# Sums of x made earlier, take-outs ahead of the curve, joined blocks in PSUM, parts in halves: one change to a retention kernel with two MLP layers

## The chip, the cores and the metric

The kernel runs on one core of one Trainium2 chip. The metric is the device time of one execution in microseconds (us). TensorE (PE) does the matmuls, VectorE (DVE), ScalarE (ACT) and GpSimd (POOL) do the elementwise work, and SyncE (SP) issues the DMAs. Each engine works through its own list of instructions in order and waits where an operand or a buffer isn't ready.

## The reference

```python
def _attn_ref(q, k, v):                      # 2 batches, 8 heads, 768 tokens, head size 64
    for t in range(S):
        state = gamma * state + einsum('bhd,bhe->bhde', k[:, :, t], v[:, :, t])
        y[:, :, t] = scale * einsum('bhd,bhde->bhe', q[:, :, t], state)

x = attn_out as 1536 tokens x 512
h = x @ w_in;  g = softplus(h);         x = g @ w_out      # layer one, 512 -> 2048 -> 512
h = x @ w_in2; g = s * relu(h)**2 + b;  y = g @ w_out2     # layer two
```
The softplus is written as max(h, 0) + log1p(exp(-|h|)). All data are float32.

## The kernel before

**Parts.** A matmul operand is kept as a high part (rounded by ScalarE) and a low part (the rest, a subtraction, mostly on GpSimd by `split`, L112 and L115); each product is three matmuls: high by high, high by low, low by high. `xh`, `xl` are the parts of x; `wh`, `wl` of the weights; `gh`, `gl` of the curve's result. The weights come as 64 bit words and are put together on VectorE (L287, L291, L296, L302) before their parts are made.

**Tiles.** The 1536 tokens are three tiles j of 512. The 2048 hidden units are 16 blocks of 128. PSUM has the banks `h`, `y` and `third` for first products, `word` for the weights, and four banks `acc` for second products, which are taken out into `xa[j]` when a tile's sum over some blocks is done. While one tile's sum is built, the one before must have left the same four banks.

**Stages.** (1) The recurrence over chunks of 128 tokens, with the first eight of twelve `step`s of layer one between its units (`early`, `mixed`). (2) The last four steps of these twelve, without recurrence. The first group of blocks is taken out by ScalarE (L412 in `take_out`), later ones are added into `xa` by VectorE (L590 in `take_2`). (3) `plain(0, P0)`: one pair of blocks, six slots (three tiles by two blocks), each a first product, its curve and a second product. (4) `second(0, p)` for three pairs: the first products of tiles 0 and 1 are made by a Strassen-like scheme with seven instead of eight half products, from sums of w (`sums_w`, `split_sums`) and sums of x; six slots again, each `part`, matmuls, `begin`, `middle`, the second products of another block (`whole`: `acc_2`, then `take_2`), `finish`. (5) Twelve ordinary steps. (6) Layer two: `plain(1, 0)` and `second(1, p)` for seven pairs.

**Sums of x.** `sum_x0` makes them for layer one: k = 1 on GpSimd in three rounds (L471), k = 2 on VectorE (L474, L475, twice as wide), k = 4 and k = 3 on VectorE, four instructions each (L465). `parts_x` makes their parts (L483 or L485, L488). They go into `xa[2]` and into two tiles called `p5` and `u2`. `all_x0` hands out one round for each `next(sums_0)`: one in each step of stage 2, k = 4 in slot 0 of `plain(0, P0)`, k = 3 in slot 1. `sum_x` is the same for layer two.

**The curve of a pair in layer one.** `begin` takes relu on ScalarE (L533), `middle` makes -2 relu(h) + h on VectorE (L545) and its softplus on ScalarE (L546), `finish` adds both on GpSimd (L554). Blocks of which one half product was kept in SBUF (`kept`, L508) are first added together by `joined` (L519).

The order on each engine is the order of the code: `tc.manual_schedule()` changes nothing in it.

Of the kernel before, what the change touches and what calls it, by code (L numbers as in the profile page):

```python
# [7 lines left out]
F32 = mybir.dt.float32  # L8
# [3 lines left out]
ALU = mybir.AluOpType  # L12
# [29 lines left out]
P0, P1 = FG // 2, PAIRS - FG // 2  # L42
# [6 lines left out]
def tile_retention_mlps(ctx: ExitStack, tc: tile.TileContext, qk, kv, w1, w2, sb, consts, out):  # L49
    nc = tc.nc  # L50
# [59 lines left out]
    def split(hi, lo, src, hi_eng, lo_eng):  # L110
        if hi_eng is nc.scalar:
            nc.scalar.activation(hi, src, AF.Copy)  # L112
        else:
            hi_eng.tensor_copy(hi, src)
        lo_eng.tensor_tensor(out=lo, in0=src, in1=hi.bitcast(F32), op=ALU.subtract)  # L115
# [210 lines left out]
    def split_sums(w):  # L326
        hi = late.tile([P, 4, KH], F32R, tag="sh", name="sh")
        lo = late.tile([P, 4, KH], F32R, tag="sl", name="sl")
        split(hi, lo, s_t[w], nc.scalar, nc.gpsimd)
        s_t[w] = (hi, lo)  # L330
        yield

# [118 lines left out]
    def sum_x0(k):  # L451

        def of(j, half):
            return [t[j][:, 2 * half : 2 * half + 2].bitcast(F32) for t in (xh, xl)]

        add, less = ALU.add, ALU.subtract
        (h11, l11), (h12, l12), (h21, l21), (h22, l22) = of(0, 0), of(1, 0), of(0, 1), of(1, 1)
        if k > 2:
            for c, tag in enumerate(("p5", "u2")):
                x3[c] = late.tile([P, TT], F32, tag=tag, name=tag)  # L460
            t, t2 = x3, x_t[2]
            todo = ((t2, h11, less), (None, l11, less)) if k == 3 else ((h21, t2, less), (None, l21, add))
            for x, y, op in todo:
                for c in range(2):
                    nc.vector.tensor_tensor(out=t[c], in0=t[c] if x is None else x[:, c], in1=y[:, c], op=op)  # L465
            return
        t = x_t[k] = xa[2][:, 2 * k - 2 : 2 * k]
        if k == 1:
            for x, y, op in ((h12, h11, less), (t, l12, add), (t, l11, less)):
                for c in range(2):  # L470
                    nc.gpsimd.tensor_tensor(out=t[:, c], in0=x[:, c], in1=y[:, c], op=op)  # L471
                yield
        else:
            nc.vector.tensor_tensor(out=t, in0=h22, in1=x_t[1], op=less)  # L474
            nc.vector.tensor_tensor(out=t, in0=t, in1=l22, op=add)  # L475
            yield

    def parts_x(k, la=1):
        hi, lo = both(k)
        if k == 3 or k == 4 and not la:  # L480
            src = [x3[c] for c in range(2)]
            for c in range(2):
                nc.scalar.activation(hi[:, c], src[c], AF.Copy)  # L483
        else:
            nc.scalar.activation(hi, x_t[k], AF.Copy)  # L485
            src = [x_t[k][:, c] for c in range(2)]
        for c in range(2):
            nc.gpsimd.tensor_tensor(out=lo[:, c], in0=src[c], in1=hi[:, c].bitcast(F32), op=ALU.subtract)  # L488
        x_t[k] = hi, lo

    def six(ps, w, x, start):
# [21 lines left out]
    def next_t():  # L513
        turn[0] ^= 1
        return tp.tile([P, TT], F32, tag="t2" if turn[0] else "t1", name="c")

    def joined(ps, t):
        c = next_t()
        nc.vector.tensor_tensor(out=c, in0=ps, in1=t, op=ALU.add)  # L519
        return c  # L520

    def begin(la, src, own=False, by_pool=True, tags=None):

        if la:
            c = src if own else next_t()
            nc.scalar.activation(c, src, AF.Relu)  # L526
            return src, c, None
        if tags:
            r, u = (late.tile([P, TT], F32, tag=tag, name=tag) for tag in tags)
        else:  # L530
            r, u = next_t(), None
        if by_pool:
            nc.scalar.activation(r, src, AF.Relu)  # L533
            return src, r, u if tags else src if own else next_t()
        nc.vector.tensor_scalar(
            out=r.bitcast(U32), in0=src.bitcast(U32), scalar1=0x80000000, scalar2=None, op0=ALU.bitwise_or
        )
        nc.scalar.activation(r, r, AF.Softplus)
        return src, r, None
# [169 lines left out]
    with tc.manual_schedule():  # L709
# [57 lines left out]
        def mixed(s):  # L767
# [18 lines left out]
                    take_out(old, cc)  # L786
            fill(2)

        for s in range(SB):
            (early if s < LAG_U else mixed)(s)  # L790
        for old in range(SB - LAG_U, SB - LAG):
            acc_mm(old, FIRST)
            acc_mm(old, SECOND)
# [13 lines left out]
        def go_first():  # L807
            if work not in sums_of_w:
                go(work, 2)
# [49 lines left out]
        def whole(acc, take):  # L859
            acc(FIRST + SECOND)  # L860
            take(FIRST + SECOND)
# [29 lines left out]
        def second(la, p):  # L891

            w = la * NF + 2 * p
            base = at[la, p + 1]
            (ah, al), (bh, bl), (sh, sl) = w_t[w, 0], w_t[w + 1, 0], s_t[w]
            a11, a12 = (ah[:, :KH], al[:, :KH]), (ah[:, KH:], al[:, KH:])
            a22 = bh[:, KH:], bl[:, KH:]
            s1, s2, s3, s4 = ((sh[:, k], sl[:, k]) for k in range(4))
            b11, b21 = ((xh[0][:, k : k + 2], xl[0][:, k : k + 2]) for k in (0, 2))
            b22 = xh[1][:, 2:4], xl[1][:, 2:4]  # L900
            t1, t2, t3, n4 = (x_t[k] for k in (1, 2, 3, 4))

            one, other, third = bank(ps_h, "h"), bank(ps_y, "y"), bank_2[1]

            part(base + 2)
            six(one, a11, b11, True)
            p1 = kept(one, "p1")
            six(third, a12, b21, True)
            c11 = begin(la, joined(third, p1), own=True)
            end_part()  # L910
            go_first()
            middle(c11)
            whole(*of_pair(la, p - 1, 1, 0))
            finish(la, p, 0, 0, c11)
            go_last()

            part(base + 3)
            six(other, s1, t1, True)
            p5 = kept(other, "p5")
            six(one, s2, t2, False)  # L920
            u2 = kept(one, "u2")
            end_part()
            go_first()
            whole(*of_pair(la, p - 1, 1, 1))
            go_last()

            part(base + 4)
            six(other, s4, b22, False)
            c12 = begin(la, joined(other, u2), own=True)
            six(one, s3, t3, False)  # L930
            c22 = begin(la, joined(one, p5), own=True)
            end_part()
            go_first()
            middle(c12)
            middle(c22)
            whole(*of_pair(la, p - 1, 2, 0))
            finish(la, p, 0, 1, c12)
            finish(la, p, 1, 1, c22)
            go_last()

            part(base + 5)
            six(one, a22, n4, False)
            c21 = begin(la, one, tags=("u2", "p1"))
            end_part()
            go_first()
            middle(c21)
            whole(*of_pair(la, p - 1, 2, 1))
            finish(la, p, 1, 0, c21)
            go_last()

            part(base + 6)
            all_of(third, (ah, al), 2)
            ha = begin(la, third)
            end_part()
            go_first()
            middle(ha)
            whole(*of_pair(la, p, 0, 0))
            finish(la, p, 0, 2, ha)
            go_last()

            part(base + 7)
            other = bank(ps_y, "y")
            all_of(other, (bh, bl), 2)
            hb = begin(la, other)
            end_part()
            go_first()
            middle(hb)
            for banks in (FIRST, SECOND) if la and p == PAIRS - 1 else (FIRST + SECOND,):
                acc_2(la, p, 0, 1, banks)
                take_2(la, p, 0, banks)  # L970
            finish(la, p, 1, 2, hb)
            go_last()

        def all_x0():
            for k in (1, 2, 4, 3):
                yield from sum_x0(k)
                if k > 2:
                    yield

        def all_x():  # L980
            for k in (1, 3, 2, 4):
                sum_x(k)
                yield

        sums_0 = all_x0()
        for s in range(SB, GS):
            accs = [of_step(s - LAG)]
            step(s, accs, at[0, P0 + 1] * (s < SB + 2), [sums_0], nc.gpsimd)
        s = GS - 1
        act_3(s)  # L990
        act_hi(s)
        act_lo(s, nc.gpsimd)
        parts_x(1, 0)
        left = [lambda s=s: whole(*of_step(s)) for s in range(GS - LAG, GS)]
        plain(0, P0, left, [[sums_0], [sums_0], [], [], [], []], [(4,), (2,), (), (3,), (), ()])
        for p in range(P0 + 1, P1):
            second(0, p)
        end_part()
# [103 lines left out]
```

## Time and profile before

| what | value |
|---|---|
| time, median of 3 runs | 585.71 us (585.37 to 586.18) |
| profiled execution: its own time, its span | 586.1 us, 584.0 us |
| PE busy in the span | 565.4 us (97%) |
| DVE, ACT, POOL busy | 411.0, 337.5, 340.8 us |
| mean granted TensorE clock | 0.993 of full speed |

The span goes from the first to the last instruction of the profile; the 2.1 us between it and the time lie outside. PE is busy nearly everywhere, so what can be won without taking matmuls away is in its 18.6 idle us and in the stretches where its clock is lowered.

### The profile page before, as it was taken

The numbers are of one execution on the slowest core, as the hardware profiler recorded it, in microseconds if no ns is written. First come the engines' busy times: TensorE is split into PE (matmuls) and PEld (weight loads), VectorE is DVE, ScalarE is ACT, GpSimd is POOL, SyncE is SP. The second block draws the span as 40 slices with busy tenths as digits, with TensorE's granted clock in tenths as the row PEclk, the third lists the DMA queues.
The fourth block names the chain that finished last, engine by engine and source line by source line (L and its number), as shares of the span: only waits on it lengthen the run. The fifth ranks groups of instructions, "written<-read, shape, count | busy, mean of one in ns | idle before, by whom it ended". The sixth has DMA issues, their size and how long they took to land.

```text
span 584.0 us, 8106 instructions
## 1 busy us (share of the span) xinstructions
PE 565.4 (97%) x2968; PEld 462.7 (79%) x2968; DVE 411.0 (70%) x619; ACT 337.5 (58%) x606; POOL 340.8 (58%) x276
## 2 busy tenths in 40 slices
PE   8899999996999999999999999999999999999997
PEld 7777778885878877788887887888888888888885
DVE  4899766497796968999697687667576665765324
ACT  4656564434554454654344697858676666667460
POOL 3447634885769696963344769756464655556030
PEclk9999999997999999999999999999999999999999
DMA  8985212102021221233210213222212122100005
GB/s 334 415 303 198 70 50 96 37 1 74 17 91 37 72 74 65 82 106 101 81 50 23 73 36 109 72 74 64 81 36 93 52 73 72 37 0 1 0 2 215
DMA packets 14870, 50.58 MB, mean 87 GB/s; under 512 B 1776, under 2 KB 1776, under 8 KB 14832
## 3 DMA queue, kind: packets, MB, share of 16 engines
q1 hardware_dynamic: 14832, 50.08, 25.0%
q8 instruction: 23, 0.38, 0.2%
q14 instruction: 15, 0.12, 0.1%
HBM read 46.93 MB, written 3.15 MB: 86 GB/s over the span
## 4 chain that ended last, share of the span: by engine, by line
PE 76%; DVE 12%; POOL 3%; ACT 3%; DMA 3%; issue 2%; DVEq 0%; SPq 0%; ACTq 0%
PE acc L580 28%; PE acc L404 10%; PE h L494 7%; PE h L353 6%; PE y L502 6%; PE third L502 4%; PE y L353 4%; PE y L494 4%; PE y L190 2%; PE third L494 2%; DMA qk<-qk 2%; DVE xa L590 2%; POOL sl L115 1%; DVE c L545 1%; PE s L174 1%
## 5 line engine op out<-in xcount | busy, mean ns | idle before, releaser
L115 POOL TENSOR_TENSOR wl<-wm,wh 128x512 fp32r<-128x512 f32 x64 | 84.8, 1325 | 109.8 <-ACT wh L112 109.8
L115 POOL TENSOR_TENSOR gl<-c,gh 128x512 fp32r<-128x512 f32 x69 | 91.2, 1323 | 87.1 <-ACT gh L112 69.1
L590 DVE TENSOR_TENSOR xa<-acc,xa 128x512 f32<-128x512 f32 x132 | 82.4, 684 | 84.2 <-PE acc L580 84.2
L580 PE MATMUL acc<-wh,gh 128*128 128x512 f32 x192 | 74.9, 390 | 0.0
L580 PE MATMUL acc<-wh,gl 128*128 128x512 f32 x192 | 74.7, 389 | 0.0
L580 PE MATMUL acc<-wl,gh 128*128 128x512 f32 x192 | 52.5, 389 | 0.0
L112 ACT ACTIVATE gh<-c 128x512 fp32r<-128x512 f32 x69 | 43.6, 632 | 11.0 <-POOL c L554 6.7
L112 ACT ACTIVATE wh<-wm 128x512 fp32r<-128x512 f32 x64 | 39.8, 622 | 15.4 <-DVE wm L302 15.3
L294 ACT ACTIVATE wm<-raw 128x512 f32<-128x512 f32 x64 | 42.3, 660 | 8.8 <-POOL wl L115 7.9
L580 PE MATMUL acc<-gh,wh 128*128 128x512 f32 x96 | 38.8, 404 | 8.3 <-ACT xa L412 5.1
L580 PEld LDWEIGHTS acc<-wh,gh 128*128 128x128 f32 x192 | 36.0, 188 | 8.2 <-DVE xa L590 0.4
L291 DVE SCALAR_TENSOR_TENSOR word<-raw,cu,word 128x512 uint32<-128x512 uint32 x54 | 40.8, 756 | 1.9
L302 DVE SCALAR_TENSOR_TENSOR wm<-wm,word 128x512 f32<-128x512 f32 x54 | 37.1, 688 | 7.0 <-ACT wm L294 1.5
L580 PEld LDWEIGHTS acc<-wl,gh 128*128 128x128 f32 x192 | 36.0, 188 | 7.5
L580 PEld LDWEIGHTS acc<-wh,gl 128*128 128x128 f32 x192 | 36.0, 188 | 7.5
L296 DVE SCALAR_TENSOR_TENSOR word<-raw,cu,word 128x512 uint32<-128x512 uint32 x54 | 40.5, 750 | 0.8
L552 ACT ACTIVATE c<-c,sbt 128x512 f32<-128x512 f32 x48 | 39.2, 817 | 1.6
L580 PE MATMUL acc<-gl,wh 128*128 128x512 f32 x96 | 38.4, 400 | 0.0
L404 PE MATMUL acc<-gh,wh 128*128 128x512 f32 x96 | 38.3, 399 | 0.0
L526 ACT ACTIVATE c<-c 128x512 f32<-128x512 f32 x21 | 13.3, 633 | 42.1 <-DVE c L519 41.5
L404 PE MATMUL acc<-gl,wh 128*128 128x512 f32 x96 | 37.5, 390 | 0.0
L287 DVE TENSOR_SCALAR word<-raw 128x512 uint32<-128x512 uint32 x54 | 37.1, 687 | 0.5
(218 smaller groups left out, 1407.8 us busy)
## 6 DMA issues: line engine op xcount, KB each, us to landing
raw<-w SPq DMA_DIRECT2D x64, 512.0 KB, 3.7
qk<-qk SPq DMA_DIRECT2D x12, 512.0 KB, 7.6
kv<-kv SPq DMA_DIRECT2D x12, 512.0 KB, 7.7
out<-xa SPq DMA_DIRECT2D x12, 256.0 KB, 2.1
cst<-consts SPq DMA_DIRECT2D x1, 518.0 KB, 4.1
cst<-consts SPq DMA_DIRECT2D x1, 256.0 KB, 5.5
sbt<-sb SPq DMA_DIRECT2D x1, 1.0 KB, 10.5
```

Of the source, the lines that this page charges most:

```text
L112: nc.scalar.activation(hi, src, AF.Copy)
L115: lo_eng.tensor_tensor(out=lo, in0=src, in1=hi.bitcast(F32), op=ALU.subtract)
L291: nc.vector.scalar_tensor_tensor(out=x, in0=hw, scalar=cu[:, 0:1], in1=x, op0=ALU.bitwise_and, op1=ALU.bitwise_or)
L294: nc.scalar.activation(m, hw.bitcast(F32), AF.Square)
L296: nc.vector.scalar_tensor_tensor(out=x, in0=lw, scalar=cu[:, 1:2], in1=x, op0=ALU.logical_shift_right, op1=ALU.bitwise_or)
L353: nc.tensor.matmul(ps, w[:, cc * P : (cc + 1) * P], r[j][:, cc, :], start=i == 0, stop=i == len(ops) - 1)
L404: nc.tensor.matmul(acc_t[la, g, j][cc], *ops[i], start=f4 == 0 and i == 0, stop=ends(s) and i == 2)
L494: nc.tensor.matmul(ps, w[a][:, k * P : (k + 1) * P], x[b][:, k], start=start and i == 0, stop=i == len(ops) - 1, skip_group_check=True,)
L502: nc.tensor.matmul(ps, w[a][:, k * P : (k + 1) * P], (xh, xl)[b][j][:, k], start=i == 0, stop=i == len(ops) - 1)
L552: nc.scalar.activation(c, c, AF.Identity, scale=sbt[:, 0:1], bias=sbt[:, 1:2])
L580: nc.tensor.matmul(acc_t[la, p, "pair", j][cc], *ops[i], start=half == 0 and i == 0, stop=half == 1 and i == 2)
L590: nc.vector.tensor_tensor(out=dst, in0=ps, in1=dst, op=ALU.add)
```

## The change

It does five things. (a) The first four rounds of the sums of x for layer one (k = 1 on GpSimd in three, k = 2 on VectorE) move from stage 2 into the last four steps with recurrence, k = 4 from slot 0 of `plain(0, P0)` into stage 2, k = 3 from slot 1 into slot 0, and the parts move with them. (b) In the fourth slot of a pair the second products with their take-out stand ahead of `middle`. (c) In layer one, two of three joined blocks stay in their PSUM bank instead of a tile in SBUF. (d) The parts of the sums of w are made in two halves. (e) In layer two the low part of the third sum of x is made by VectorE instead of GpSimd.

```diff
--- before.py
+++ after.py
@@ -326,7 +326,8 @@
     def split_sums(w):
         hi = late.tile([P, 4, KH], F32R, tag="sh", name="sh")
         lo = late.tile([P, 4, KH], F32R, tag="sl", name="sl")
-        split(hi, lo, s_t[w], nc.scalar, nc.gpsimd)
+        for o in (slice(0, 2), slice(2, 4)):
+            split(hi[:, o], lo[:, o], s_t[w][:, o], nc.scalar, nc.gpsimd)
         s_t[w] = (hi, lo)
         yield
 
@@ -458,7 +459,7 @@
         if k > 2:
             for c, tag in enumerate(("p5", "u2")):
                 x3[c] = late.tile([P, TT], F32, tag=tag, name=tag)
-            t, t2 = x3, x_t[2]
+            t, t2 = x3, xa[2][:, 2:4]
             todo = ((t2, h11, less), (None, l11, less)) if k == 3 else ((h21, t2, less), (None, l21, add))
             for x, y, op in todo:
                 for c in range(2):
@@ -484,8 +485,9 @@
         else:
             nc.scalar.activation(hi, x_t[k], AF.Copy)
             src = [x_t[k][:, c] for c in range(2)]
+        eng = nc.vector if la and k == 3 else nc.gpsimd
         for c in range(2):
-            nc.gpsimd.tensor_tensor(out=lo[:, c], in0=src[c], in1=hi[:, c].bitcast(F32), op=ALU.subtract)
+            eng.tensor_tensor(out=lo[:, c], in0=src[c], in1=hi[:, c].bitcast(F32), op=ALU.subtract)
         x_t[k] = hi, lo
 
     def six(ps, w, x, start):
@@ -514,8 +516,8 @@
         turn[0] ^= 1
         return tp.tile([P, TT], F32, tag="t2" if turn[0] else "t1", name="c")
 
-    def joined(ps, t):
-        c = next_t()
+    def joined(ps, t, here=False):
+        c = ps if here else next_t()
         nc.vector.tensor_tensor(out=c, in0=ps, in1=t, op=ALU.add)
         return c
 
@@ -786,8 +788,17 @@
                     take_out(old, cc)
             fill(2)
 
+        def all_x0():
+            for k in (1, 2, 4, 3):
+                yield from sum_x0(k)
+                if k > 2:
+                    yield
+
+        sums_0 = all_x0()
         for s in range(SB):
             (early if s < LAG_U else mixed)(s)
+            if s >= SB - 4:
+                next(sums_0)
         for old in range(SB - LAG_U, SB - LAG):
             acc_mm(old, FIRST)
             acc_mm(old, SECOND)
@@ -906,7 +917,7 @@
             six(one, a11, b11, True)
             p1 = kept(one, "p1")
             six(third, a12, b21, True)
-            c11 = begin(la, joined(third, p1), own=True)
+            c11 = begin(la, joined(third, p1, not la), own=bool(la))
             end_part()
             go_first()
             middle(c11)
@@ -926,7 +937,7 @@
 
             part(base + 4)
             six(other, s4, b22, False)
-            c12 = begin(la, joined(other, u2), own=True)
+            c12 = begin(la, joined(other, u2, not la), own=bool(la))
             six(one, s3, t3, False)
             c22 = begin(la, joined(one, p5), own=True)
             end_part()
@@ -943,8 +954,8 @@
             c21 = begin(la, one, tags=("u2", "p1"))
             end_part()
             go_first()
+            whole(*of_pair(la, p - 1, 2, 1))
             middle(c21)
-            whole(*of_pair(la, p - 1, 2, 1))
             finish(la, p, 1, 0, c21)
             go_last()
 
@@ -971,28 +982,22 @@
             finish(la, p, 1, 2, hb)
             go_last()
 
-        def all_x0():
-            for k in (1, 2, 4, 3):
-                yield from sum_x0(k)
-                if k > 2:
-                    yield
-
         def all_x():
             for k in (1, 3, 2, 4):
                 sum_x(k)
                 yield
 
-        sums_0 = all_x0()
         for s in range(SB, GS):
             accs = [of_step(s - LAG)]
-            step(s, accs, at[0, P0 + 1] * (s < SB + 2), [sums_0], nc.gpsimd)
+            step(s, accs, at[0, P0 + 1] * (s < SB + 2), [sums_0] * (s == SB + 2), nc.gpsimd)
+            if s != SB + 2:
+                parts_x((1, 2, None, 4)[s - SB], 0)
         s = GS - 1
         act_3(s)
         act_hi(s)
         act_lo(s, nc.gpsimd)
-        parts_x(1, 0)
         left = [lambda s=s: whole(*of_step(s)) for s in range(GS - LAG, GS)]
-        plain(0, P0, left, [[sums_0], [sums_0], [], [], [], []], [(4,), (2,), (), (3,), (), ()])
+        plain(0, P0, left, [[sums_0], [], [], [], [], []], [(), (3,), (), (), (), ()])
         for p in range(P0 + 1, P1):
             second(0, p)
         end_part()
```

On VectorE, at the border of stage 2 and `plain(0, P0)`: the rows of before from the sums of k = 2 to slot 2's first curve step (`c<-third`), with k = 4 left out at the three dots. `p`, `u` are the two tiles of k = 3, `c<-h`, `c<-y`, `c<-third` the curves of slots 0, 1, 2.

```order
L474 TENSOR_TENSOR xa_111<-xh_104,xa_111 128x1024
L475 TENSOR_TENSOR xa_111<-xa_111,xl_107 128x1024
L535 TENSOR_SCALAR c<-h 128x512
L558 SCALAR_TENSOR_TENSOR c<-h,c 128x512
...
L535 TENSOR_SCALAR c<-y 128x512
L558 SCALAR_TENSOR_TENSOR c<-y,c 128x512
L465 TENSOR_TENSOR p_1434<-xa_111,xh_103 128x512
L465 TENSOR_TENSOR u_1435<-xa_111,xh_103 128x512
L465 TENSOR_TENSOR p_1434<-p_1434,xl_106 128x512
L465 TENSOR_TENSOR u_1435<-u_1435,xl_106 128x512
L535 TENSOR_SCALAR c<-third 128x512
```

The same place after the change:

```order
L361 TENSOR_SCALAR t_1339<-y 128x512
L371 SCALAR_TENSOR_TENSOR t_1354<-y,t_1339 128x512
L537 TENSOR_SCALAR c<-h 128x512
L560 SCALAR_TENSOR_TENSOR c<-h,c 128x512
L466 TENSOR_TENSOR p_1406<-xa_111,xh_103 128x512
L466 TENSOR_TENSOR u_1407<-xa_111,xh_103 128x512
L466 TENSOR_TENSOR p_1406<-p_1406,xl_106 128x512
L466 TENSOR_TENSOR u_1407<-u_1407,xl_106 128x512
L537 TENSOR_SCALAR c<-y 128x512
L560 SCALAR_TENSOR_TENSOR c<-y,c 128x512
L537 TENSOR_SCALAR c<-third 128x512
```

The four sums that stood directly ahead of slot 2's curve now stand a slot earlier, and the wide sums of k = 2 are gone from here.

On VectorE, in slots three and four of the first pair of layer one, before (`xa<-acc` are the take-outs, `p<-u,h` is `middle` of slot four):

```order
L519 TENSOR_TENSOR c<-y,u_1675 128x512
L519 TENSOR_TENSOR c<-h,p_1667 128x512
L287 TENSOR_SCALAR word<-raw 128x512
L291 SCALAR_TENSOR_TENSOR word<-raw,cu,word 128x512
L545 SCALAR_TENSOR_TENSOR c<-c 128x512 x2
...
L545 SCALAR_TENSOR_TENSOR p_1769<-u_1768,h 128x512
L590 TENSOR_TENSOR xa_111<-acc_1741,xa_111 128x512 x2
```

and after:

```order
L521 TENSOR_TENSOR y<-y,u_1677 128x512
L521 TENSOR_TENSOR c<-h,p_1669 128x512
L287 TENSOR_SCALAR word<-raw 128x512
L291 SCALAR_TENSOR_TENSOR word<-raw,cu,word 128x512
L547 SCALAR_TENSOR_TENSOR c<-c,y 128x512
L547 SCALAR_TENSOR_TENSOR c<-c 128x512
...
L592 TENSOR_TENSOR xa_111<-acc_1743,xa_111 128x512 x2
L592 TENSOR_TENSOR xa_111<-acc_1744,xa_111 128x512
L592 TENSOR_TENSOR xa_111<-acc_1745,xa_111 128x512
L547 SCALAR_TENSOR_TENSOR p_1771<-u_1770,h 128x512
```

One of the two curve steps of slot three now reads the bank `y`, and the take-outs of slot four have passed that slot's curve step.

On VectorE, from the end of `plain(1, 0)` to the first pair of layer two, after the change (`x3l` is the low part of the third sum, `c<-third,p` the first joined block of the pair):

```order
L302 SCALAR_TENSOR_TENSOR wm<-wm,word 128x512
L490 TENSOR_TENSOR x3l<-p_3117,x3h 128x512
L490 TENSOR_TENSOR x3l<-u_3119,x3h 128x512
L521 TENSOR_TENSOR c<-third,p_3369 128x512
L287 TENSOR_SCALAR word<-raw 128x512
```

The two `x3l` rows are new in this list; before, they stood on GpSimd behind the `wl` that follows the last curve of `plain(1, 0)`. PE's list is the same row for row.

## Rows read from the trace of the kernel before

**Rows 1.** The page, first part: busy time of PE.

```profile
PE 565.4 (97%) x2968; PEld 462.7 (79%) x2968; DVE 411.0 (70%) x619; ACT 337.5 (58%) x606; POOL 340.8 (58%) x276
```

**Rows 2.** Waits: engine, line, releaser; us in total, times, longest us.

```profile
PE acc L580 <- ACT xa L412: 5.1, 1, 5.1
PE acc L580 <- DVE xa L590: 3.3, 3, 1.1
PE y L494 <- ACT p L508: 1.3, 1, 1.3
```

**Rows 3.** Chain that ended last, around PE's gaps: start us, us, what.

```profile
137.90 5.06 PE acc L580 x12
142.97 2.72 PE third L502 x12
...
175.36 2.99 PE acc L580 x12
```

**Rows 4.** Stretch behind the longest gap: us; PE, PEld, DVE, ACT, POOL; clock, DMA.

```profile
137.90:143.00 5.10, 5.10 (x13) 4.08 (x14) 3.61 (x6) 4.09 (x8) 3.45 (x4) 0.57 0.48 151
```

**Rows 5.** Timeline of ACT, slot 2: start us, us, instruction, idle before.

```profile
134.26 0.63 ACT L538 ACTIVATE c<-c 128x512 f32<-128x512 f32 x1 [5.36 <-DVE c L535]
...
136.79 2.04 ACT L412 ACTIVATE xa<-acc 128x512 f32<-128x512 f32 x4
```

**Rows 6.** Timeline of DVE: a sum beside an idle and beside a busy POOL.

```profile
123.95 0.68 DVE L465 TENSOR_TENSOR p<-p,xl 128x512 f32<-128x512 f32 x1
...
131.79 1.77 DVE L465 TENSOR_TENSOR u<-u,xl 128x512 f32<-128x512 f32 x1
```

**Rows 7.** Timelines of POOL, PE and DVE where the sums come to stand.

```profile
68.80 1.29 POOL L159 TENSOR_TENSOR q<-qk,cst 128x512 f32<-128x512 f32 x1
...
77.03 0.66 PE L190 MATMUL y<-q,st 128*64 128x128 f32 x8
...
94.81 0.69 DVE L360 TENSOR_SCALAR t<-h 128x512 uint32<-128x512 uint32 x1 [0.64 <-PE h L353]
...
102.77 0.39 PE L353 MATMUL h<-xh,wh 128*128 128x512 f32 x1
```

**Rows 8.** Timeline of DVE, slots three and four of the first pair.

```profile
168.06 2.39 DVE L545 SCALAR_TENSOR_TENSOR c<-c 128x512 f32<-128x512 f32 x2
...
173.33 0.68 DVE L545 SCALAR_TENSOR_TENSOR p<-u,h 128x512 f32<-128x512 f32 x1
173.93 2.48 DVE L590 TENSOR_TENSOR xa<-acc,xa 128x512 f32<-128x512 f32 x4
...
177.81 0.68 DVE L545 SCALAR_TENSOR_TENSOR c<-c,third 128x512 f32<-128x512 f32 x1
```

**Rows 9.** Timelines of POOL and PE, from that slot to the next pair.

```profile
168.08 1.82 POOL L115 TENSOR_TENSOR wl<-wm,wh 128x512 fp32r<-128x512 f32 x1 [4.92 <-ACT wh L112]
...
176.57 1.28 POOL L554 TENSOR_TENSOR u<-u,p 128x512 f32<-128x512 f32 x1
...
187.78 2.40 POOL L115 TENSOR_TENSOR sl<-ws,sh 128x1024 fp32r<-128x1024 f32 x1
...
189.74 0.39 PE L494 MATMUL y<-x1l,sh 128*128 128x512 f32 x1
190.23 0.73 PE L494 MATMUL y<-x1h,sl 128*128 128x512 f32 x2
```

**Rows 10.** Timelines of POOL, DVE and ACT at layer two's first pair.

```profile
352.38 2.56 POOL L488 TENSOR_TENSOR x4l<-xa,x4h 128x512 fp32r<-128x512 f32 x2
...
353.37 0.69 DVE L302 SCALAR_TENSOR_TENSOR wm<-wm,word 128x512 f32<-128x512 f32 x1
...
355.48 0.63 ACT L526 ACTIVATE c<-c 128x512 f32<-128x512 f32 x1 [0.76 <-DVE c L519]
...
357.48 0.67 ACT L294 ACTIVATE wm<-raw 128x512 f32<-128x512 f32 x1 [0.85 <-POOL wl L115]
...
360.09 0.58 ACT L508 ACTIVATE p<-y 128x512 f32<-128x512 f32 x1
```

## The prediction, made before the changed kernel was run

> **What bounds the kernel now.** I read the page first: PE is busy 97% of the span [rows 1], so only its gaps and its slow stretches can give time. Then the waits of PE: the longest is one of 5.1 us on a take-out by ScalarE, next come three of 1.1 us on take-outs by VectorE, then one of 1.3 us in layer two on a copy by ScalarE [rows 2]. Then the chain that ended last, to see what a gap costs behind it: twelve matmuls take 2.72 us in plain running, 5.06 us behind the long gap, and 2.99 us behind a gap of 1.1 us [rows 3]. [...] So the long gap costs 5.1 + (5.06 - 2.72) = 7.4 us, and each short one 1.1 + (2.99 - 2.72) = 1.4 us. The reader is to see that PE's own work, which the change leaves as it is, fills all the rest.
>
> **Sums of x (part a).** Why are ScalarE's take-outs late? They start at 136.79, and their list is held from 134.26 on by a softplus that waited 5.36 us for VectorE's first curve step of slot 2 [rows 5]. VectorE was at the sums of k = 3: the last of the four ran from 131.79 to 133.49 and took 1.77 us, where the same operation takes 0.68 us beside an idle POOL [rows 6]. Both engines were subtracting between SBUF tiles, and such steps take turns: 1.77 is about a POOL step (1.29, [rows 7]) plus a VectorE step. After the change these four stand one slot earlier, and the wide sums of k = 2 have left the place too. Slot 2's first product ends at about 127.4, two times 2.72 ahead of PE's stop at 132.8 = 137.90 - 5.1 [rows 2, 3]. From the softplus's start to PE's restart 137.90 - 134.26 = 3.6 us pass [rows 3, 5]; with VectorE's step of 0.7 us ahead of it, started at 127.4 to 128.6 (the second, if a last sum still has to finish in turns with POOL), the banks are free at 131.7 to 132.9. PE asks at 132.8. I take the whole gap as gone: **-7.4 us**; if a sum is left in front, up to 1.8 us of wait comes back (one turn of 1.77).
>
> What the moved work costs where it goes. On POOL three rounds of two subtractions (two times 1.29 = 2.6 us) come ahead of the next chunk's scaled q in two steps and behind it in one. That q starts at 68.80 and is read at 77.03 [rows 7]: it would be ready at 72.7, 4.4 us early. On VectorE the sums of k = 2 stand ahead of step 8's first curve step, which started at 94.81 [rows 7]. They can start when that queue is free at about 94.1; two twice as wide steps (two times 1.2) in turns with one POOL step (1.3) are done by about 97.7, so the step's curve is 3 us later and its bank is free at about 100.3. PE wants it at 102.77 [rows 7]; 2.5 us are left, and later steps catch up: a step has at most six VectorE instructions of about 0.7 us beside 5.44 us of matmuls (two twelves). No new DMA is issued, and the loads of words follow the same list. I count **0** here, with PE's own work as the cover; without it each microsecond late would be a microsecond.
>
> **The pair's slots (parts b, c, d).** VectorE works without a gap from 168.06 to the take-outs at 173.93, whose first two free the banks for which PE waits until 175.36 [rows 3, 8]. Ahead of them the change takes away one curve step (173.33 to 173.93: 0.60 us), and one of the two at 168.06 no longer reads two SBUF tiles. These two took 2.39 us together, while the POOL step at 168.08 took 1.82 instead of about 1.29 [rows 8, 9]: VectorE, POOL, VectorE in turns. With one of them out of the turns, POOL starts at once and VectorE is done 0.55 us earlier, at 169.9 instead of 170.45. Together 1.15 us, and the wait was 1.1: it goes. What the in-place sum in PSUM costs the trace doesn't show; a curve step with one operand in PSUM takes 0.68 us, the same as one out of SBUF beside an idle POOL [rows 6, 8], so I take nothing, between -0.1 and +0.2 a pair. [...]
>
> Not all of 1.4 us is kept in each pair. The curve step that the take-outs pass is now late: its softplus lets POOL's addition start at about 176.5, as before [rows 9], while PE is 1.4 us earlier. From there POOL works nearly without a break to the low parts of the sums of w at 187.78 to 190.18, and PE already waits for these: a matmul that could follow at 189.97 (189.74 and a twelfth of 2.72) starts at 190.23 [rows 3, 9]. In halves, the first is ready after half of 2.40, at 189.0, and PE goes on at about 189.1 by this clock: 1.13 to 1.25 us ahead of before. So two pairs give 1.25 and the third, behind which no such sum comes, 1.4: **-3.9 us**. At least 1.7 of it (three times 0.55, from the turns alone) is to come, and at most 3 x 1.4 + 2 x 0.26 = 4.7. In layer two, no pair shows a wait on these parts, and halving them adds about 0.1 us on ScalarE and POOL in each, under PE's work: 0.
>
> **Low part of the third sum in layer two (part e).** The 1.3 us wait there ends on a copy by ScalarE at 360.09, at the end of a list held up twice: by the joined block of VectorE (0.76 us, ended at 355.48) and by POOL (0.85 us, ended at 357.48) [rows 10]. The two subtractions come off POOL behind the step for which ScalarE waits, so that wait isn't shortened. On VectorE they come ahead of the joined block. VectorE gets to them at about 354.0, after the step at 353.37; POOL is then in the second of its two steps, which ends at 354.94 [rows 10]. The first subtraction runs after it, to 355.5; POOL's next step takes its turn to 356.8; the second runs to 357.4. The joined block is then done at about 358.0, and ScalarE starts at 358.1 instead of 355.48. From there to the copy its own work is 3.7 us (360.09 - 355.48 less the 0.85 of waiting, which is over by then), so the copy starts at 361.75 instead of 360.09: **+1.65 us**. Bounds: -1.6 (the wait of 1.3 and 0.3 of slow matmuls behind it gone), and +1.65 + 2.0, if the gap of then 2.9 us lowers the clock as the one of 5.05 did (2.3 us behind it, against 0.3 behind those of 1.1); I take the price of the nearer rows, 0.3, which is paid already.
>
> **The sum.** 586.1 (the profiled execution's own time) - 7.4 - 3.9 + 1.65 = 576.4 us. The median of the runs is 0.4 below that execution, so I say 576.2.
>
> **The rivals.** (1) As forecast, 575.0 to 577.6: 55 in 100. (2) The subtractions on VectorE fall beside an idle POOL or ahead of ScalarE's need, and layer two's wait stays or goes: 586.1 - 7.4 - 3.9 - (0 to 1.6) = 573.2 to 574.8. Against it stands that POOL has no break in that stretch: 13. (3) The pairs keep half of their waits, because the in-place sum or the later curve step is longer than I count: 3.9 shrinks to 1.7 to 2.7, 577.6 to 578.6: 14. (4) Layer two's longer gap lowers the clock: 578.4: 8. (5) A sum is still ahead of slot 2's curve: +1.8 and, if the clock drops, 2.3 more, 578.2 to 580.5. It needs VectorE to be 1.2 us later than I count at 127.4: 6. (6) Slower than before: VectorE's list blocks at k = 2, whose first operand is POOL's third round. I have that ready at about 91 (68.80 and 2.6, and two more steps of the recurrence, each 9.7 us by the chain), against 94.1. POOL would have to be later by 3, then by the 2.5 us of the bank, and from there each microsecond adds one and the clock 2.3: it ends above 585.7 from about 12 us of lateness on, say at 587. Nothing on POOL in that stretch is that long: 2. (7) The change doesn't move the long wait, because the take-outs wait for something else than VectorE's list: about 583.8 (586.1 - 3.9 + 1.65), or no change if the pairs don't gain either: 2.
>
> **How the numbers follow.** The time is that of (1). From 573.0 to 580.0 the range holds (1) to (4) and most of (5), which is more than 8 in 10; cases that I haven't thought of are the rest. A measurement of this kernel tells 0.2% (1.2 us) from no change. Faster: all but (6) and half of (7), 0.96; the same: 0.02; slower: 0.02.
>
> **What would show it.** The long wait of PE on the ScalarE take-out is gone from its waits, the granted clock is full between 130 and 145, and the sums' four steps on VectorE end before slot 2's product. The three waits on the VectorE take-outs are under 0.3 us, and two waits of about 0.4 us on the first half of the low parts of the sums of w stand in the second and third pair. In layer two's first pair the two subtractions on VectorE take about 1.7 us each, and PE's wait for the copy is longer, about 2.9 us. The prediction is wrong if PE shows a new gap in the recurrence, if the take-outs of the pairs still come late, or if that last wait is shorter than before.

## The result and the profile after

The changed kernel takes 577.53 us (median of 4 runs, 576.74 to 578.23), the one before in the same rounds 585.67 us: a ratio of 0.986, with a 95% interval of 0.9842 to 0.9878. It is faster, inside the range, and 1.3 us above the forecast. Its profiled execution took 578.15 us with a span of 576.4.

The page, first part, and the longest waits of PE (us in total, times, longest), beside [rows 1, 2]:

```profile
PE 564.4 (98%) x2968; PEld 461.7 (80%) x2968; DVE 412.0 (71%) x621; ACT 338.3 (59%) x616; POOL 337.9 (59%) x284
```

```profile
PE y L496 <- ACT p L510: 2.8, 1, 2.8
PE h L354 <- DVE t L371: 1.8, 3, 0.8
```

PE's waits on both kinds of take-outs are gone from this list. The one in layer two, 1.3 us before, is 2.8. The chain that ended last, beside [rows 3] (start us, us, what; x12 are twelve matmuls):

```profile
132.75 2.72 PE acc L582 x12
135.47 2.72 PE third L504 x12
...
230.73 2.91 PE acc L582 x12
...
236.36 2.90 PE acc L582 x12
...
351.53 1.65 PE y L496 x6
353.18 2.56 PE h L496 x6
355.74 3.14 PE acc L582 x12
```

And the stretches where slot 2 meets the first group's take-outs, and behind layer two's wait (us; PE, PEld, DVE, ACT, POOL; clock, DMA), beside [rows 4]:

```profile
130.00:137.00 7.00, 7.00 (x33) 5.79 (x32) 5.43 (x9) 4.93 (x9) 4.24 (x4) 1.00 0.25 77
...
352.00:362.00 10.00, 10.00 (x39) 8.05 (x38) 4.78 (x7) 6.48 (x11) 5.91 (x8) 0.83 0.20 66
```

The reader is to see two things. Twelve matmuls now start at 132.75 and take 2.72 us where they started at 137.90 and took 5.06, at a granted clock of 1.00 where it was 0.57. And a lowered clock turns up at a new place: behind layer two's wait six matmuls take 2.56 us instead of 1.36, and twelve 3.14 instead of 2.72, at 0.83.

Where the time went, by starts of the same work in both traces. From the chain of before, the fourth-slot accumulations of the second and third pair and layer two's y with the six matmuls behind it (start us, us, what):

```profile
208.38 3.01 PE acc L580 x12
...
241.47 3.00 PE acc L580 x12
...
360.72 1.67 PE y L494 x6
362.39 1.39 PE h L494 x6
```

And PE's timeline after, the first matmul of that accumulation in each of the three pairs (the chain lists the last of them at 230.73):

```profile
166.74 0.47 PE L582 MATMUL acc<-gh,wh 128*128 128x512 f32 x1
...
198.70 0.47 PE L582 MATMUL acc<-gh,wh 128*128 128x512 f32 x1
...
230.66 0.47 PE L582 MATMUL acc<-gh,wh 128*128 128x512 f32 x1
```

From 45 us on, ahead of the moved sums, PE's work already runs 0.10 us earlier, which the change didn't do. The matmuls behind the long wait: third product 142.97 to 135.47, less that 0.10, **-7.40**. The pairs: the first fourth-slot accumulation 175.36 to 166.74, of which 7.50 stood already, -1.12; its period from pair to pair, 33.02 and 33.09 before and 31.96 twice after, -1.06 and -1.13; and behind the third one 0.15 lost on the way out (8.43 us from that accumulation to stage 5's first product, 8.28 before): **-3.16**. The ordinary steps up to layer two: -0.06. Layer two up to its y: **+1.53**. The slow matmuls behind it: **+1.57**. With the 0.10 that is -7.62; the spans, 584.0 and 576.4, differ by 7.6.

### The profile page after: what moved, and what is told of

It reads as the page before. It is cut to its first block, busy times and chain, and to the rows that moved or that the text cites. A ratio compares the mean times of both kernels' runs of the same rounds, so it can differ in the third digit from the quotient of the medians.

```text
span 576.4 us, 8120 instructions
## 1 busy us (share of the span) xinstructions
PE 564.4 (98%) x2968; PEld 461.7 (80%) x2968; DVE 412.0 (71%) x621; ACT 338.3 (59%) x616; POOL 337.9 (59%) x284
## 4 chain that ended last, share of the span: by engine, by line
PE 77%; POOL 5%; DVE 5%; DMA 5%; ACT 5%; issue 2%; SPq 0%; DVEq 0%; POOLq 0%
PE acc L582 27%; PE acc L405 11%; PE h L496 8%; PE h L354 6%; PE y L504 5%; PE third L504 5%; PE y L496 4%; PE y L354 4%; DMA qk<-qk 3%; PE y L190 2%; DMA raw<-w 2%; PE third L496 2%; POOL c L556 2%; PE h L504 1%; POOL gl L115 1%
## 5 line engine op out<-in xcount | busy, mean ns | idle before, releaser
L294 ACT ACTIVATE wm<-raw 128x512 f32<-128x512 f32 x64 | 42.1, 658 | 7.1 <-POOL wl L115 7.0
L405 PE MATMUL acc<-gh,wh 128*128 128x512 f32 x96 | 38.3, 399 | 0.0
L582 PE MATMUL acc<-gh,wh 128*128 128x512 f32 x96 | 37.6, 392 | 0.0
```

Of the source, the lines that this page charges most:

```text
L294: nc.scalar.activation(m, hw.bitcast(F32), AF.Square)
L405: nc.tensor.matmul(acc_t[la, g, j][cc], *ops[i], start=f4 == 0 and i == 0, stop=ends(s) and i == 2)
L582: nc.tensor.matmul(acc_t[la, p, "pair", j][cc], *ops[i], start=half == 0 and i == 0, stop=half == 1 and i == 2)
```

## The experiments

The kernel before was run beside each group of runs; its median was 585.67 us beside the changed kernel, 586.18 beside the first four experiments, 586.09 beside the next four and 585.83 beside the last two.

**Without the low part on VectorE (e).** The changed kernel with:

```diff
-        eng = nc.vector if la and k == 3 else nc.gpsimd
+        eng = nc.gpsimd
```

> The changed kernel with the low part of layer two's third sum back on GpSimd (part e undone). Theory: the two subtractions on VectorE, in turns with GpSimd, put off the joined block, and with it the copy by ScalarE for which PE waits 2.79 us. Without them the wait is 1.25 us again, the clock stays full behind it, and the time is 577.5 - 1.5 - 0.8 (half of the runs pay 1.5 us for the clock) = 575.2 us, 574.5 to 575.7. Rival: the wait there comes from ScalarE's own full list, which the halves have made longer; then it stays above 2.3 us and the time stays within 0.5 us of 577.5.

Measured: 575.40 us (575.13 to 575.59), ratio 0.9821 (0.9808 to 0.9834). PE's wait and what follows it:

```profile
PE y L496 <- ACT p L510: 1.4, 1, 1.4
```

```profile
349.98 1.66 PE y L496 x6
351.63 1.36 PE h L496 x6
```

The theory holds: part (e) makes the kernel slower, and the kernel without it beats the changed one. The wait is half as long, and the second six matmuls behind it take 1.36 us.

**Part (a) alone.** The kernel before with the moved sums and their parts, without (b) to (e):

```diff
+            if s >= SB - 4:
+                next(sums_0)
...
-        plain(0, P0, left, [[sums_0], [sums_0], [], [], [], []], [(4,), (2,), (), (3,), (), ()])
+        plain(0, P0, left, [[sums_0], [], [], [], [], []], [(), (3,), (), (), (), ()])
```

> The kernel before with the sums of x moved, and nothing else (part a alone). Theory: the gap of 5.05 us and the slow clock behind it go, worth 7.4 us, so 585.7 - 7.4 = 578.3 us, 577.8 to 578.8; the three waits of 1.1 us on VectorE's take-outs and the 1.25 us in layer two stay. Rival: the moved sums also take time from the pairs or the recurrence; then PE shows waits there that the kernel before hasn't, and the time is above 579.

Measured: 578.62 us (578.39 to 578.84), ratio 0.9876 (0.9861 to 0.9892). The pairs' waits stay as they were:

```profile
PE acc L581 <- DVE xa L591: 3.3, 3, 1.1
...
PE y L495 <- ACT p L509: 1.2, 1, 1.2
```

The theory holds: (a) brings 7.1 us by itself against the 585.67 of the changed kernel's own comparison, and 7.6 against the 586.18 beside this run. The changed kernel's median is another 1.1 lower, since (e) gives back much of what (b), (c) and (d) bring.

**Part (e) alone.** The kernel before with the line of the first experiment the other way round (VectorE for k = 3 in layer two):

> The kernel before with only part e (low part of layer two's third sum on VectorE). Theory: PE's wait for the copy grows from 1.25 to about 2.8 us and the clock falls behind it in some runs by 1.5 us more: 585.7 + 1.5 to 3.1, so 587.2 to 588.8 us, slower. Rival: relieving GpSimd pays there, 584.5 to 585.7.

Measured: 587.67 us (586.76 to 591.04, 12 runs), ratio 1.0041 (1.0026 to 1.0057): slower by 0.4%, as in the theory. In its profiled run (586.83 us) the wait is 2.6 us, and the matmuls behind it ran at full clock:

```profile
361.69 1.66 PE y L495 x6
363.35 1.36 PE h L495 x6
364.71 2.72 PE acc L581 x12
```

The spread is wider than the theory's. Four of the twelve runs took 589.77 to 591.04 us at a mean clock of 0.987 to 0.991, lower than the 0.993 to 0.997 of the kernel before beside them. No such run was profiled, so where they lose it isn't shown.

**Without part (b).** The changed kernel with the take-outs behind the curve's step again:

```diff
-            whole(*of_pair(la, p - 1, 2, 1))
             middle(c21)
+            whole(*of_pair(la, p - 1, 2, 1))
```

> The changed kernel with the take-outs of slot four behind the curve step again (part b undone). Theory: VectorE gets to the take-outs 0.60 us later, so PE waits about 0.6 us in each of three pairs; GpSimd's addition is about 0.4 us earlier, so the waits on the first half of the low parts of the sums of w, 0.23 us each in the second and third pair, go. Time 577.5 + 3 x 0.6 - 2 x 0.25 = 578.8 us, 578.2 to 579.2. Rival: GpSimd's chain from pair to pair is the limit, not VectorE's list; then the order in the slot is worth nothing in the first two pairs and the time is 577.5 to 578.1.

Measured: 578.83 us (577.39 to 579.10), ratio 0.9875 (0.9859 to 0.989). PE waits again for the take-outs, half as long as before:

```profile
PE acc L582 <- DVE xa L592: 1.7, 3, 0.6
```

Of the 1.3 us between the medians a part is the clock of the runs that each happened to have. Run for run at the same mean clock it is 577.39 against 576.74 and 576.92 at 1.0, and 578.76 to 579.10 against 578.15 and 578.23 at 0.996 and 0.997: (b) is worth 0.6 to 0.7 us. So the median meets the theory's 578.8 by the clock, and the theory's 1.3 us is twice what (b) gives. Its waits of 0.53 to 0.59 us in each pair are there. But what goes in return is more than it counted: by PE's matmul starts, the 0.36 and 0.34 us lost on the first half of sl, and 0.10 to 0.18 behind the low part of slot four's curve (c21). The first two pairs gain only about 0.1 us each from (b), the third 0.4. That is near the rival, in which GpSimd's chain is the limit in the first two pairs.

**Without part (d).** The changed kernel with the sums' parts made whole:

```diff
-        for o in (slice(0, 2), slice(2, 4)):
-            split(hi[:, o], lo[:, o], s_t[w][:, o], nc.scalar, nc.gpsimd)
+        split(hi, lo, s_t[w], nc.scalar, nc.gpsimd)
```

> The changed kernel with split_sums writing each part of the sums whole, as before, and not in halves. The theory (the halves matter, since with a shorter pair TensorE reaches the sums' parts sooner): TensorE waits for the whole of sl, about 1.25 us more in the second and in the third pair, so 577.5 + 2.5 = 580.0 us (579.4 to 580.5). The rival (the halves only took the 0.26 us that the trace of before shows): 577.5 to 578.2 us.

Measured: 579.80 us (579.04 to 580.44), ratio 0.9889 (0.9873 to 0.9905). The wait is there, in two pairs:

```profile
PE y L495 <- POOL sl L115: 2.2, 2, 1.1
```

At a clock of 1.0 its runs took 579.04 and 579.20 us, 2.3 more than the changed kernel's 576.74 and 576.92 at that clock. The theory holds. The trace of before shows only 0.26 us of this wait each [rows 3, 9]: it grows as the rest of the pair gets shorter.

**Without part (c).** The changed kernel with the joined blocks in SBUF:

```diff
-            c11 = begin(la, joined(third, p1, not la), own=bool(la))
+            c11 = begin(la, joined(third, p1), own=True)
...
-            c12 = begin(la, joined(other, u2, not la), own=bool(la))
+            c12 = begin(la, joined(other, u2), own=True)
```

> The changed kernel with the joined blocks of the pairs written to SBUF again, the rest kept. The theory (joined blocks in PSUM spare the curve's steps the turns that VectorE and GpSimd take on SBUF): about 0.55 us more in the chain of each pair ahead of the low part of c21 and the first half of sl, on which TensorE already waits, so 577.5 + 1.65 = 579.2 us (578.5 to 579.7). The rival (the addition in PSUM costs what it spares): within 0.4 us of 577.5.

Measured: 580.35 us (580.18 to 580.81), ratio 0.9901 (0.9885 to 0.9916). VectorE's two curve steps of a pair's third slot and the POOL step that starts with them, here in the second pair:

```profile
193.27 2.38 DVE L547 SCALAR_TENSOR_TENSOR c<-c 128x512 f32<-128x512 f32 x2
...
193.29 1.81 POOL L115 TENSOR_TENSOR wl<-wm,wh 128x512 fp32r<-128x512 f32 x1 [3.42 <-ACT wh L112]
```

In the changed kernel they take 0.68 and 1.20 us and the POOL step 1.30. PE's period from pair to pair is 32.51 here (167.46, 199.97, 232.49) and 31.96 with (c): 0.55 us a pair, as in the theory. The median lies above the theory's range, because all four runs had a clock of 0.997; the changed kernel's runs at such a clock took 578.15 to 579.06, and the difference to their median (578.33 of six, the last experiment's with them) is 2.0.

**x3's parts in slot 1 of layer two's first pair.** The changed kernel without (e), and with the parts of the third sum of x moved:

```diff
-        eng = nc.vector if la and k == 3 else nc.gpsimd
+        eng = nc.gpsimd
...
-        plain(1, 0, left, [[sums_1], [], [sums_1], [sums_1], [], []], [(1,), (), (), (2,), (4,), (3,)])
+        plain(1, 0, left, [[sums_1], [], [sums_1], [sums_1], [], []], [(1,), (3,), (), (2,), (4,), ()])
```

> The changed kernel without the low part of x3 on VectorE (so 575.4 us), and with layer two's parts of x3 made in slot 1 instead of slot 2, where ScalarE and GpSimd idle. The theory (TensorE's last wait of 1.4 us ahead of layer two's y is set by ScalarE's full list ahead of the copy p): the list is 1.04 us shorter and the wait 0 to 0.4 us, so 574.0 us (573.6 to 574.6). The rival (GpSimd's low part of the curve sets it as well): 575.2 to 575.5 us.

Measured: 575.93 us (575.49 to 576.13), ratio 0.9822 (0.9809 to 0.9835); the wait stays at 1.4. ScalarE, freed of the work, stands still instead, for a POOL step that frees the weight tile:

```profile
344.76 0.62 ACT L112 ACTIVATE wh<-wm 128x512 fp32r<-128x512 f32 x1
347.17 0.68 ACT L294 ACTIVATE wm<-raw 128x512 f32<-128x512 f32 x1 [1.79 <-POOL wl L115]
...
349.78 0.58 ACT L510 ACTIVATE p<-y 128x512 f32<-128x512 f32 x1
```

The theory falls and the rival holds in kind: POOL's list sets the copy p. The median is 0.4 us above the rival's range and 0.5 above the kernel without (e), so this move alone gains nothing.

**The two take-outs on both sides of the curve's step.** The kernel of the experiment before, and in a pair's fourth slot:

```diff
-            whole(*of_pair(la, p - 1, 2, 1))
+            acc, take = of_pair(la, p - 1, 2, 1)
+            acc(FIRST + SECOND)
+            take(FIRST)
             middle(c21)
+            take(SECOND)
```

> The kernel with x3's parts in slot 1, and in each pair's fourth slot the first take-out ahead of the curve's step and the second behind it. The theory (what each pair still loses, 0.18 us on the low part of c21 and 0.23 us on the first half of sl, comes of the curve's step standing behind both take-outs): the step comes 1.2 us sooner, these waits go, so about 1.0 us less than the kernel with x3's parts in slot 1, near 573.0 us (572.5 to 573.6). The rival (the second take-out, now behind the step, makes the next accumulation wait, as in the kernel without that part of the change): equal to it or up to 1.3 us slower.

Measured: 575.50 us (575.11 to 576.02), ratio 0.9816 (0.9803 to 0.9829): no difference that these runs can tell. Its chain shows a gain and a loss:

```profile
166.76 3.37 PE acc L582 x12
170.13 2.75 PE y L504 x12
172.88 2.72 PE acc L582 x12
...
198.72 3.29 PE acc L582 x12
```

In the first pair the accumulation in slot 6 no longer waits for the low part of c21 (2.72, in the kernel without this edit 2.89), but the one in slot 4 takes 3.37 where it took 2.97; its last two banks are emptied later. By PE's matmul starts the period is 31.89 and 31.87 us here, 31.96 and 31.97 there: the two orders differ by under 0.1 us a pair. The theory falls; "equal to it", as the rival has it, holds.

**x4's parts later.** The kernel with x3's parts in slot 1, and:

```diff
-        plain(1, 0, left, [[sums_1], [], [sums_1], [sums_1], [], []], [(1,), (3,), (), (2,), (4,), ()])
+        plain(1, 0, left, [[sums_1], [], [sums_1], [sums_1], [], []], [(1,), (3,), (), (2,), (), (4,)])
```

> The kernel with x3's parts in slot 1 (the low part on GpSimd), and x4's parts moved from slot 4 of layer two's first pair to its last slot, behind the generated weights' parts there. The theory (the last wait of 1.4 us is set by GpSimd's full list: x4's low part, 2.56 us, stands ahead of the two low parts of which the second frees the weight tile that ScalarE writes ahead of the copy p): ScalarE goes on about 1.8 us sooner, the wait is 0 to 0.2 us, and the kernel takes about 1.3 us less than the one with x3's parts in slot 1, 574.6 us (574.1 to 574.9). The rival (the copy waits for something behind GpSimd, as VectorE's weight word or TensorE's own order): the wait stays over 1 us and the time within 0.3 us of that kernel.

Measured: 573.79 us (573.41 to 573.98), ratio 0.9787 (0.9771 to 0.9803): the fastest here. The wait on p is no longer among PE's waits; ScalarE writes the weight tile at once, the copy is done before PE asks:

```profile
344.81 0.66 ACT L294 ACTIVATE wm<-raw 128x512 f32<-128x512 f32 x1
...
347.41 0.58 ACT L510 ACTIVATE p<-y 128x512 f32<-128x512 f32 x1
```

```profile
348.37 0.39 PE L496 MATMUL y<-xh,sh 128*128 128x512 f32 x1
```

The theory holds in its mechanism, and its size is too small. The time is 2.1 us below the kernel without this edit, where the theory said 1.3. In the traces an accumulation ahead of x4's parts, where the edit does nothing yet, already starts 0.48 us earlier (332.21 and 332.69), and the last one 2.19 (556.63 and 558.82). The edit's share is 1.71: the wait of 1.4, and the 0.3 by which six matmuls behind it took 1.66 instead of 1.36.

**The changed kernel once more.**

> The changed kernel itself once more, for the share of its runs in which the clock falls behind its wait of 2.8 us in layer two. The theory (the fall comes in some runs and not in others, and costs about 1.5 us): its runs stand in two groups, near 576.8 us at a mean clock of 1.0 and near 578.2 us at 0.996 or 0.997, with nothing between. The rival (the 1.4 us between them in the first four runs come from elsewhere): times spread over 576.7 to 578.3 us without regard to the clock.

Measured: 578.39 us (578.31 to 579.06), ratio 0.9869 (0.9849 to 0.9889), all four runs at a mean clock of 0.997, the profiled one with a wait of 2.7 us and 0.84 in the stretch behind it. With the first four runs there are now two at a clock of 1.0 (576.74, 576.92) and six at 0.996 or 0.997 (578.15 to 579.06), and nothing between them: the theory holds.

## Why the prediction was right, and where it was off

**Sums of x: right.** -7.4 forecast, -7.40 measured. VectorE's last sum and the curve of slot 1 behind it, then ScalarE's softplus of slot 2 and its take-outs, which empty the four banks:

```profile
123.54 0.68 DVE L466 TENSOR_TENSOR u<-u,xl 128x512 f32<-128x512 f32 x1
124.14 0.68 DVE L537 TENSOR_SCALAR c<-y 128x512 uint32<-128x512 uint32 x1
...
128.14 0.63 ACT L540 ACTIVATE c<-c 128x512 f32<-128x512 f32 x1 [0.17 <-DVE c L537]
...
130.73 2.04 ACT L413 ACTIVATE xa<-acc 128x512 f32<-128x512 f32 x4
```

The four sums end at 124.22, ahead of slot 2's product, the softplus starts at 128.14, and the last bank is free at 132.77, in the forecast's 131.7 to 132.9. So rival (5), a sum still in front, didn't come, nor did (7). What the sums cost in the recurrence was worked out as well: POOL's q is ready at 72.67 (72.7 forecast), the sum of k = 2 ends at 97.74 (97.7), and PE shows no new wait there (rival 6):

```profile
71.20 1.47 POOL L159 TENSOR_TENSOR q<-qk,cst 128x512 f32<-128x512 f32 x1
...
95.54 2.20 DVE L476 TENSOR_TENSOR xa<-xa,xl 128x1024 f32<-128x1024 f32 x1
```

**The pair's slots: right in kind, -3.16 instead of -3.9.** The long waits on the take-outs went, and the turns with POOL fell away as forecast: VectorE's two steps end 1.87 us after they start instead of 2.39, and POOL's step takes 1.29 instead of 1.82 [rows 8, 9]:

```profile
160.56 0.68 DVE L547 SCALAR_TENSOR_TENSOR c<-c,y 128x512 f32<-128x512 f32 x1
161.16 1.27 DVE L547 SCALAR_TENSOR_TENSOR c<-c 128x512 f32<-128x512 f32 x1
...
165.31 2.48 DVE L592 TENSOR_TENSOR xa<-acc,xa 128x512 f32<-128x512 f32 x4
167.71 0.68 DVE L547 SCALAR_TENSOR_TENSOR p<-u,h 128x512 f32<-128x512 f32 x1
```

Beside that POOL step (160.59 to 161.88) the step that reads the bank `y` takes 0.68 us, and the one between SBUF tiles 1.27, to 162.43. The runs with and without (c) agree, with 0.55 us a pair between them.

The size was off in the third pair above all: 1.4 forecast, 1.13 - 0.15 = 0.98 kept; the first two kept 1.12 and 1.06 instead of 1.25. The step that failed is "the wait was 1.1: it goes", with the slow matmuls behind it: counted from the end of the product ahead of it, the slot's accumulation still takes 2.99, 2.93 and 2.91 us in the three pairs, not 2.72. Its first matmul starts 0.09 to 0.15 us late. In the first pair the profile puts its weight load's wait down to a ScalarE step (L294), but VectorE's second take-out ends at about the same time, 166.6 (an estimate from four take-outs in 2.48 us from 165.31 on), so which of the two holds it stays open. And I followed the passed curve step's lateness to the sums' halves alone, but its own low part comes late first: POOL's addition waits for the softplus, then the low part for ScalarE's high part, and PE loses 0.10, 0.11 and 0.18 us on it in slot 6 of the three pairs (2.90 instead of 2.72 in the third).

```profile
169.13 1.30 POOL L556 TENSOR_TENSOR u<-u,p 128x512 f32<-128x512 f32 x1 [0.51 <-ACT p L548]
171.17 1.29 POOL L115 TENSOR_TENSOR gl<-u,gh 128x512 fp32r<-128x512 f32 x1 [0.74 <-ACT gh L112]
...
180.34 2.57 POOL L115 TENSOR_TENSOR sl<-ws,sh 128x512 fp32r<-128x512 f32 x2
```

In the first two pairs these losses shorten the later wait on the first half of sl, 0.23 us (a matmul that could follow at 181.47 starts at 181.70) instead of the forecast 0.4, so there they cost less. The experiment with the take-outs on both sides shows that the loss in slot 6 can go only for more in slot 4. Parts (b), (c) and (d), taken out singly, are worth 0.6 to 0.7, 1.7 to 2.0 and 2.1 to 2.3 us, more in sum than the 3.16 of all three: the waits stand in one chain, and the return of one hides part of the others, as the experiment without (b) shows. What the halves of (d) cost is near the forecast's 0.1: over the ten sums of w, the two halves of sl take POOL 2.56 us together in the mean where the whole took 2.41, and those of sh take ScalarE 1.16 where it took 1.05.

**The third sum's low part: right, +1.53 instead of +1.65.** (By its own terms the forecast is +1.7: 358.1 and 3.7 are 361.8.) First VectorE's two subtractions and the joined block, then ScalarE's start and the copy:

```profile
343.23 1.69 DVE L490 TENSOR_TENSOR x3l<-p,x3h 128x512 fp32r<-128x512 f32 x1
344.84 1.78 DVE L490 TENSOR_TENSOR x3l<-u,x3h 128x512 fp32r<-128x512 f32 x1
346.54 0.68 DVE L521 TENSOR_TENSOR c<-third,p 128x512 f32<-128x512 f32 x1
...
347.26 0.63 ACT L528 ACTIVATE c<-c 128x512 f32<-128x512 f32 x1 [3.16 <-DVE c L521]
...
350.90 0.58 ACT L510 ACTIVATE p<-y 128x512 f32<-128x512 f32 x1
```

They take turns with POOL, 1.7 and 1.8 us each, where such a step took 0.68 beside an idle POOL [rows 6], and POOL's two steps beside them and the joined block take 1.74 each instead of about 1.3; the joined block waits for both, and the wait is 2.8 (2.9 forecast). Rival (2) is refuted by two runs, (e) taken away and (e) alone.

**The price of that longer gap: wrong.** The step is "I take the price of the nearer rows, 0.3, which is paid already". The gap of 2.8 us lowered the clock in the profiled run and cost 1.57 us; rival (4) had this at 8 in 100, with 578.4. By the mean clock it came in six of the changed kernel's eight runs. The forecast is that of the two runs without it, 576.74 and 576.92, and these lie 0.5 to 0.7 above it, about the 0.74 of the pairs less the 0.12 of layer two. From the forecast of 576.4 for the profiled run to its 578.15: pairs +0.74, layer two -0.12, clock +1.57, the start and the rest of the span -0.16, and what lies outside the span 1.75 instead of 2.1, -0.35, in sum 1.7.

That the median of 577.53 us still lies in rival (1)'s 575.0 to 577.6 is luck: two of the first four runs happened to stand at either level, and it is the middle between them. The median of all eight runs is 578.27, next to the 578.4 of rival (4).

That the low mean clock of the other runs is the same stretch is argued from the profiled ones, not shown in each. Five runs with a mean clock of 0.996 or 0.997 were profiled (the changed kernel twice, and it without (b), (c) and (d)); in each the clock from 352 to 362 us is 0.83 or 0.84.

## What to carry to other kernels

A step that gives one engine relief is paid for where it lands: ask first which list the waiting engine's releaser stands in, and move work off that list, not off the one that looks fullest; here moving x4's parts further back in POOL's own list won 1.7 us, and moving x3's low part to VectorE lost 1.4 to 2.9. When several waits stand in one chain, give each removal the size up to the next limit, look for every consumer of what has been pushed back, and take parts out singly to see what each is worth. A TensorE gap between two known prices is to be costed at both, with real chances, and runs of the kernel are to be compared at the same clock.

## What the runs showed of the hardware

A gap can be followed by a lowered clock in some runs and not in others. With 2.6 to 2.8 us in layer two and no longer gap elsewhere (the changed kernel, and it without (b), (c) or (d)), 15 of 20 runs had a mean clock of 0.996 or 0.997, and 5 had 1.0; within one kernel the two levels lie 1.3 to 1.5 us apart. With 1.2 to 1.4 us there (the kernels without (e)), none of 18 runs fell below 0.999, and the four without this gap had the same. The profiled run of (e) alone, with 2.6 us, went on at full clock. The kernel before, with its gap of 5.1 us, has two levels as well: of the 17 runs beside the first four experiments, 5 had a mean clock of 0.996 or 0.997 (median 585.28 us) and 12 one of 0.993 or 0.994 (586.34). The profiled one, from which the 7.4 us are read, had 0.993; where the others differ from it isn't shown. What decides in a run which of the two levels it takes isn't shown either.

An in-place sum in PSUM costs VectorE no more than 0.01 us here: in the pairs of layer one `joined` into the banks `third` and `y` takes 0.70 and 0.69 us, and into SBUF, in the kernel before, 0.69 and 0.68.
